# The first two batches of an attention and feed-forward kernel: TensorE's order written out by hand, and SyncE's order of loads

## The chip, the cores and the metric

The kernel runs on one core of a Trainium2 chip. The metric is the device time of one execution in microseconds (us). Before the change it is 924.86 us, the median of 3 runs (923.78 to 927.17). The profiled execution took 924.03 us, and its span in the trace is 922.2 us; the 1.83 us between them lie around the span.

## The reference

For 8 batches of 8 heads (sequence 576, head size 64), attention with two kinds of mask, and then a feed-forward layer over all 4608 tokens:

```python
scores = scale * np.matmul(q, k.transpose(0, 1, 3, 2))
mask_local = (rel >= 0) & (rel < 32)
mask_strided = (rel >= 0) & (pos[None, :] % 32 == pos[:, None] % 32)
# heads 0 to 3: local, heads 4 to 7: strided; softmax over the keys
attn_out = np.matmul(attn, v)
h = x @ w_in                 # x: 4608 x 512, w_in: 512 x 2048
out = (h * np.cos(h)) @ w_out
```

Everything is float32. The products of the feed-forward layer are made from numbers split into a high and a low part, so that one exact product takes three matmuls.

## The kernel before

**The feed-forward layer** works on blocks of 384 tokens and on 16 slices (`f`) of the hidden size. For a block `j` and a slice `f`, `hidden` makes 12 matmuls into bank `a` or `b` (L476), then the cosine curve on ScalarE and VectorE (L482 to L489: scaling, reduction, sine, multiplication by h), then the split into `g_hi` and `g_lo`. `outer` multiplies these with `w_out` in 9 matmuls (L500), three steps (`LAG`) later. Blocks 0 and 1 are worked on together, slice by slice, as their weights arrive; blocks 2 to 5 follow with the attention of batches 2 to 7 laid between their steps; blocks 6 to 11 go through another form (L772, L801).

**The weights** come as 32 tiles of 512 KB (`load_weight`, L144: `raw`, three buffers), two for each slice. ScalarE, VectorE (L158, L161, L167) and GpSimd (L172) turn each into a high and a low part. The n-th load stands behind the load of attention unit 4 + n in SyncE's queue. `put_away` (L591) writes parts of them back to DRAM in 80 stores (L596, L604), for use in the last six blocks.

**The attention** goes in units. A batch has seven: strided, strided, local, strided, strided, local, local (`units`, L422). Here u0 to u6 are the units of batch 0 and u7 to u13 those of batch 1. One unit is: a load of q and k (L297, L352; three buffers `qk`) and of v (L293, L356; five buffers); on TensorE a matmul that lays down the mask (L234) and the score matmuls (L307 local, L367 strided), into one of three banks in turn; the softmax (VectorE L249, L250, ScalarE exponential L261, VectorE L274 to L276, GpSimd L278); a transposition (strided: TensorE L387 and a ScalarE copy L391; local: VectorE L317); the products with v (TensorE L336 local, L401 strided); and copies and splits of the result (`keep`: ScalarE L432, GpSimd L433). Block 0 needs batch 0 alone; block 1 also needs u7, u8, u9, u10 and u11.

**What sets the order.** A scheduler goes through the program with modelled times and puts each engine's instructions into one fixed queue. It takes what is ready in its model and goes by the order of the program otherwise; `order(later, first, ...)` adds an edge that holds the two in sequence. In the attention of batches 0 and 1 (`plain`) TensorE's matmuls have no such edges: `in_stages` and `stage` (L528, L539) only say in which order the program names the stages. Small matmuls on zeros (`keep_busy`, L620, counts in `BUSY`) stand behind the scores of a step. For blocks 0 and 1 the matmuls have no edges either; from block 2 on all matmuls are chained in program order (`in_turn`). SyncE issues all loads and stores named here.

Of the kernel before, what the change touches and what calls it, by code (L numbers as in the profile page):

```python
# [13 lines left out]
F32 = mybir.dt.float32  # L14
# [8 lines left out]
B, H, S, D = 8, 8, 576, 64  # L23
# [22 lines left out]
VL = (LU + 1) * D  # L46
# [11 lines left out]

WEIGHTS_AT, WEIGHTS_EACH = 4, 1

BUSY = (10, 6, 5, 3, 2, 2, 2) + 8 * (1,)


# [23 lines left out]
def attention_cos_ffn(ctx, tc, qkl, vl, qkvs, w_in, w_out, eye, eye16, mask_l0, mask_l, mask_s, out):  # L87
# [114 lines left out]
    class Attention:  # L202
# [6 lines left out]
        def __init__(self, stack, plain, scores, transposed, products, ld_bufs):  # L209

            self.plain = plain
            self.pe = (lambda mm: mm) if plain else in_turn
            self.ld, self.wk = (
                stack.enter_context(tc.tile_pool(name=name, bufs=bufs, side="right", reuse_waits="tile"))
                for name, bufs in (("ld", ld_bufs), ("wk", 2))
            )
            self.scores, self.transposed, self.products = (
                itertools.cycle(kind) for kind in (scores, transposed, products)
            )
            self.turns, self.kept = itertools.cycle(range(len(scores))), {}  # L220
            self.pn_s = itertools.cycle(pn_s)
            self.x_t, self.copied = {}, None
# [5 lines left out]
        def score_bank(self, mask):  # L228


            if self.plain:
                bank = self.bank(self.scores)
                n, w = mask.shape[1:]
                nc.tensor.matmul(  # L234
                    bank[:, :n * w].rearrange("p (t w) -> p t w", w=w), ident16, mask, start=True, stop=False,
                    skip_group_check=True,
                )
                return bank
            n = next(self.turns)
            if n not in self.kept:  # L240
                self.kept[n] = self.bank(self.scores)
                nc.vector.memset(self.kept[n], 0.0)
            return self.kept[n]
# [39 lines left out]
        def stage(self, key):  # L283

            if key not in self.x_t:
                self.x_t[key] = self.wk.tile([P, S], F32, name="x_t")
            return self.x_t[key]

        def local(self, b, u):

            def load_v():
                v = self.ld.tile([P, max(VL, VS)], F32, name="v", bufs=5 if self.plain else 3)
                nc.sync.dma_start(out=v[:, :VL], in_=vl[b, u])  # L293
                return v

            qk = self.ld.tile([P, max(QKL, QS + KS)], F32, name="qk")
            loads.append(nc.sync.dma_start(out=qk[:, :QKL], in_=qkl[b, u]))  # L297
            if self.plain:
                v = load_v()
            q_t = qk[:, :2 * LQ].rearrange("p (h q) -> p h q", h=2)  # L300
# [3 lines left out]

            def score(t, c):
                p, j = divmod(c, 2)
                self.scored = self.pe(nc.tensor.matmul(  # L307
                    s_ps[quarter_of(c), t * KW:(t + 1) * KW], q_t[half(j), p, QB * t:QB * (t + 1)],
                    k_t[half(j), p, QB * t:QB * t + KW], start=not self.plain, stop=True, skip_group_check=True,
                ))  # L310
# [19 lines left out]
            def product(m, c):  # L330


                p, j = divmod(c, 2)
                lo, hi = max(m - 1, 0), min(m + 1, LU)
                at = m * KW - QB if m else 0
                self.pe(nc.tensor.matmul(  # L336
                    a_ps[p][half(j), lo * QB:hi * QB], v_t[quarter_of(c), m], pt[quarter_of(c), at:at + (hi - lo) * QB],
                    start=m == turns[0], stop=m == turns[-1], skip_group_check=True,
                ))
# [9 lines left out]
        def strided(self, b, p, u):  # L349
            real = min(SU, NG - SU * u)  # L350
            qk = self.ld.tile([P, max(QKL, QS + KS)], F32, name="qk")
            loads.append(nc.sync.dma_start(out=qk[:, :QS + KS], in_=qkvs[b, p, u, :, :QS + KS]))  # L352

            def load_v():
                v = self.ld.tile([P, max(VL, VS)], F32, name="v", bufs=5 if self.plain else 3)
                nc.sync.dma_start(out=v[:, :real * D], in_=qkvs[b, p, u, :, QS + KS:QS + KS + real * D])  # L356
                return v

            if self.plain:
# [4 lines left out]
            s_ps = self.score_bank(mask)  # L364

            def score(t, i):
                self.scored = self.pe(nc.tensor.matmul(  # L367
                    s_ps[half(1 - i, GB), t * GB:(t + 1) * GB], q_t[half(i), t], k_t[half(i), t],
                    start=not self.plain, stop=True, skip_group_check=True,
                ))  # L370
# [13 lines left out]
            v_t = v[:, :VS].rearrange("p (t d) -> p t d", d=D)  # L384
            t_ps = self.bank(self.transposed)
            for t in range(0, SU, 2):
                self.pe(nc.tensor.transpose(  # L387
                    t_ps[:, t * GP:(t + 2) * GP], pn[:, t:t + 2].rearrange("p t k -> p (t k)"), ident
                ))
            pt = self.wk.tile([P, SU * GB], F32, name="pt", bufs=2)  # L390
# [7 lines left out]

            def product(t, j):
                at = (t ^ 1) * GB  # L400
                self.pe(nc.tensor.matmul(  # L401
                    a_ps[half(j), t * GB:(t + 1) * GB], v_t[half(j, GB), t], pt[half(j, GB), at:at + GB], start=True,
                    stop=True, skip_group_check=True,
                ))
# [64 lines left out]

    hiddens = itertools.count()  # L470

    def hidden(j, f, x_hi, x_lo):
        h = ps_h.tile([P, 512], F32, name="ab"[next(hiddens) % 2])[:, :TB]
        ops = [(w, x, c) for c in range(NKC) for w, x in ((wi_h, x_hi), (wi_h, x_lo), (wi_l, x_hi))]
        for i, (w, x, c) in enumerate(ops):
            mm = nc.tensor.matmul(h, w[f][:, c], x[c], start=(i == 0), stop=(i == len(ops) - 1))  # L476
            if j >= 2:
                in_turn(mm)

        r = rp.tile([P, TB], F32, name="r")  # L480
# [6 lines left out]
        if j == 0 and f == 0:  # L487
            order(sin, exps[-1], "one change of tables")
        chain["curve"] = nc.vector.tensor_tensor(out=r, in0=r, in1=h, op=ALU.mult)  # L489
        g_hi = gp.tile([P, TB], F32R, name="g_hi")  # L490
        g_lo = gp.tile([P, TB], F32R, name="g_lo")
        chain["cast"] = nc.scalar.copy(out=g_hi, in_=r)  # L492
# [31 lines left out]

    def accumulators(pool):
        return [pool.tile([P, DM], F32, name=f"acc{t}") for t in range(NTT)]

    def in_stages(units, knots, lag):  # L528


        begun = np.interp(range(len(units)), [n for _, n in knots], [at for at, _ in knots]).astype(int).tolist()
        steps = {}
        for n, (at, unit) in enumerate(zip(begun, units)):
            second = min([at + lag] + begun[n + 2:n + 3])
            for stage in (at, second, second + 1):
                steps.setdefault(stage, []).append(unit)
        return steps

    def stage(unit):  # L539

        matmuls = next(unit)
        if matmuls:
            for matmul in matmuls[0]:
                matmul()
            next(unit, None)

    def burst(multiplied, scored):

# [41 lines left out]

    def put_away():  # L591

        for q in range(NQ):
            for i, f, k in ((1, q, 0), (2, q, 1), (5, q + NQ, 1)):
                for part, w in enumerate((wi_h, wi_l)):
                    nc.sync.dma_start(  # L596
                        out=wis[q][i][:, part],
                        in_=w[f][:, 2 * k:2 * k + 2].bitcast(F32).rearrange("p c n -> p (c n)"),
                    )
                if i != 2:  # L600
                    yield
            for f in (q, q + NQ):
                for part, w in enumerate((wo_h, wo_l)):
                    nc.sync.dma_start(out=wos[f][:, part], in_=w[f].bitcast(F32))  # L604
                yield

    direct = {j: x_operands() for j in range(2)}
    with ExitStack() as loading:
        cv = loading.enter_context(tc.tile_pool(name="cv", bufs=3, reuse_waits="tile"))
        with ExitStack() as stack:  # L610
# [3 lines left out]
                stack, True, ((ps_h, "a"), (ps_h, "b"), (ps, "acc0")), ((ps_o, "acc0"), (ps_o, "acc1")),  # L614
                ((ps_o, "acc2"), (ps, "acc3")), ld_bufs=3,
            )
            steps = in_stages(att.units(0) + att.units(1), ((0, 0), (20, 20)), 2)
            spare = ps.tile([P, 512], F32, name="acc2")

            def keep_busy(n, after):  # L620
                for _ in range(n):
                    mm = nc.tensor.matmul(
                        spare[:64], warm, warm.unsqueeze(1).broadcast_to([P, 8, 64]), start=True, stop=True
                    )
                    if after is not None:
                        order(mm, after, "in its place")
                    after = mm

            keep_busy(BUSY[0], None)
            for n in range(max(steps) + 1):  # L630
                for unit in steps.get(n, ()):
                    stage(unit)
                if n + 1 < len(BUSY):
                    keep_busy(BUSY[n + 1], att.scored)

        rp = ctx.enter_context(tc.tile_pool(name="rp", bufs=2, side="right", reuse_waits="tile"))
        gp = ctx.enter_context(tc.tile_pool(name="gp", bufs=LAG + 1, side="right", reuse_waits="tile"))

        with ExitStack() as stack:
# [325 lines left out]
```

## Time and profile before

| | us |
|---|---|
| median of 3 runs | 924.86 |
| profiled execution | 924.03 |
| its span | 922.2 |
| TensorE (PE) busy | 899.3 |
| VectorE (DVE) busy | 525.9 |
| ScalarE (ACT) busy | 520.3 |
| GpSimd (POOL) busy | 434.1 |

Busy times are of the whole span. In rows of engine work, the first number is the start in us from the span's start, the second the duration (of a merged run of instructions), and a bracket at the end gives the engine's idle time just before and what ended it. PEclk is the granted TensorE clock as a share of 2.4 GHz; 0.50 is 1.2 GHz.

### The profile page before, as it was taken

How to read it: one execution, taken by the hardware profiler on the slowest of the kernel's cores; microseconds unless marked ns; L12 is line 12 of the kernel's file. 1: busy time of each engine (PE TensorE's matmuls, PEld its weight loads, DVE VectorE, ACT ScalarE, POOL GpSimd, SP SyncE). 2: the span in 40 equal slices, each digit the busy share in tenths (PEclk: the TensorE clock that was granted, in tenths of full speed). 3: DMA queues.
4: the chain of work that ended last, by engine and by line, in shares of the span. 5: the costliest groups of instructions: out<-in, count | busy, mean ns of one | idle time of the engine just before them, and what ended most of it. 6: DMA issues, size and time to landing. Idle time of an engine off the chain costs nothing. (4 is left out here: it accounts for less than half of the span.)

```text
span 922.2 us, 20559 instructions
## 1 busy us (share of the span) xinstructions
PE 899.3 (98%) x7876; PEld 790.0 (86%) x7876; DVE 525.9 (57%) x1018; ACT 520.3 (56%) x1090; POOL 434.1 (47%) x466
## 2 busy tenths in 40 slices
PE   8789999999999999999999999999999999999998
PEld 5568999988888888888888888999898998999896
DVE  5658665446657666666664345646464555544453
ACT  3556777556567666656655544545555555544443
POOL 2636655544666666656746523424333434323231
PEclk9889999999999999999999999999999999999999
DMA  8938876322336535544355755756576655755401
GB/s 307 309 100 300 267 234 216 125 88 77 118 128 193 188 132 165 194 150 142 130 176 173 259 178 168 228 175 215 191 265 200 199 187 182 253 183 193 138 23 68
DMA packets 93265, 166.33 MB, mean 180 GB/s; under 512 B 10736, under 2 KB 34032, under 8 KB 93168
## 3 DMA queue, kind: packets, MB, share of 16 engines
q1 hardware_dynamic: 85248, 157.72, 52.1%
q10 hardware_dynamic: 7920, 7.31, 2.4%
q8 instruction: 62, 1.02, 0.4%
q14 instruction: 35, 0.29, 0.1%
HBM read 125.40 MB, written 39.58 MB: 179 GB/s over the span
## 5 line engine op out<-in xcount | busy, mean ns | idle before, releaser
L787 POOL TENSOR_TENSOR g_lo<-r,g_hi 128x384 fp32r<-128x384 f32 x96 | 98.8, 1029 | 247.7 <-ACT g_hi L786 139.3
L493 POOL TENSOR_TENSOR g_lo<-r,g_hi 128x384 fp32r<-128x384 f32 x96 | 103.5, 1078 | 186.1 <-ACT g_hi L492 108.8
L500 PE MATMUL acc<-s,g_hi 128*128 128x512 f32 x576 | 180.0, 396 | 0.0
L801 PE MATMUL acc<-s,g_hi 128*128 128x512 f32 x576 | 179.7, 393 | 0.0
L500 PEld LDWEIGHTS acc<-s,g_hi 128*128 128x128 f32 x576 | 105.3, 188 | 15.5
L801 PEld LDWEIGHTS acc<-s,g_hi 128*128 128x128 f32 x576 | 106.2, 188 | 10.8
L801 PE MATMUL acc<-s,g_lo 128*128 128x512 f32 x288 | 112.8, 392 | 0.0
L500 PE MATMUL acc<-s,g_lo 128*128 128x512 f32 x288 | 110.9, 390 | 0.0
L476 PE MATMUL b<-x_hi,s 128*128 128x384 f32 x384 | 109.3, 345 | 1.1 <-DVE r L489 1.1
L781 DVE SCALAR_TENSOR_TENSOR r<-r,h 128x384 f32<-128x384 int32 x96 | 58.3, 607 | 90.9 <-ACT r L780 90.8
L476 PE MATMUL a<-x_hi,s 128*128 128x384 f32 x384 | 109.2, 345 | 0.7 <-DVE r L489 0.7
L772 PE MATMUL a<-s,s 128*128 128x384 f32 x384 | 83.1, 338 | 0.0
L783 DVE TENSOR_TENSOR r<-r,h 128x384 f32<-128x384 f32 x96 | 69.9, 728 | 22.0 <-ACT r L782 20.3
L782 ACT ACTIVATE r<-r,biases 128x384 f32<-128x384 f32 x96 | 59.2, 617 | 36.8 <-DVE r L781 36.5
L486 ACT ACTIVATE r<-r,biases 128x384 f32<-128x384 f32 x96 | 58.8, 612 | 30.3 <-DVE r L483 28.5
L476 PEld LDWEIGHTS b<-x_hi,s 128*128 128x128 f32 x384 | 70.9, 190 | 4.6 <-DVE r L489 1.9
L786 ACT CAST g_hi<-r 128x384 fp32r<-128x384 f32 x96 | 49.1, 512 | 44.0 <-DVE r L783 43.6
L476 PEld LDWEIGHTS a<-x_hi,s 128*128 128x128 f32 x384 | 70.4, 188 | 3.6 <-DVE r L489 1.0
L780 ACT ACTIVATE r<-h 128x384 int32<-128x384 f32 x96 | 50.4, 525 | 39.9 <-DVE h L850 26.3
L772 PEld LDWEIGHTS a<-s,s 128*128 128x128 f32 x384 | 69.4, 188 | 4.2
L492 ACT CAST g_hi<-r 128x384 fp32r<-128x384 f32 x96 | 49.1, 511 | 29.9 <-DVE r L489 27.9
L476 PE MATMUL b<-x_lo,s 128*128 128x384 f32 x192 | 64.8, 338 | 0.0
(141 smaller groups left out, 1757.9 us busy)
## 6 DMA issues: line engine op xcount, KB each, us to landing
s<-wis SPq DMA_DIRECT2D x168, 256.0 KB, 2.9
s<-wos SPq DMA_DIRECT2D x96, 256.0 KB, 3.5
qk<-in_qkvs SPq DMA_DIRECT2D x32, 324.0 KB, 3.6
qk<-in_qkl SPq DMA_DIRECT2D x24, 416.0 KB, 3.9
out<-o SPq DMA_DIRECT2D x36, 256.0 KB, 2.4
raw<-in_w_in SPq DMA_DIRECT2D x16, 512.0 KB, 5.6
raw<-in_w_out SPq DMA_DIRECT2D x16, 512.0 KB, 3.9
wos<-s SPq DMA_DIRECT2D x32, 256.0 KB, 5.4
```

Source lines behind the costliest of these rows:

```text
L476: mm = nc.tensor.matmul(h, w[f][:, c], x[c], start=(i == 0), stop=(i == len(ops) - 1))
L486: sin = nc.scalar.activation(out=r, in_=r, func=AF.Sin, bias=quarter)
L492: chain["cast"] = nc.scalar.copy(out=g_hi, in_=r)
L493: chain["rest"] = nc.gpsimd.tensor_tensor(out=g_lo, in0=r, in1=g_hi.bitcast(F32), op=ALU.subtract)
L500: mm = nc.tensor.matmul(acc[t], g[:, ts], w[f], start=(f == 0 and i == 0), stop=(f == NFC - 1 and i == 2))
L772: in_turn(nc.tensor.matmul(bank, w[:, n, c], part, start=start and i == 0, stop=stop and i == len(ops) - 1, skip_group_check=True,))
L780: nc.scalar.activation(out=k, in_=h, func=AF.Copy, scale=1.0 / (2.0 * math.pi), bias=0.25)
L781: nc.vector.scalar_tensor_tensor(out=r, in0=k, scalar=-2.0 * math.pi, in1=h, op0=ALU.mult, op1=ALU.add)
L782: nc.scalar.activation(out=r, in_=r, func=AF.Sin, bias=quarter)
L783: chain["curve"] = nc.vector.tensor_tensor(out=r, in0=r, in1=h, op=ALU.mult)
L787: chain["rest"] = nc.gpsimd.tensor_tensor(out=g_lo, in0=r, in1=g_hi.bitcast(F32), op=ALU.subtract)
L801: in_turn(nc.tensor.matmul(acc, g[gn][:, ts], w[wn], start=done == 0 and i == 0, stop=done == NFC - 1 and i == 2,))
```

## The change

TensorE's matmuls of the first two batches are all chained with `in_turn`, the small matmuls on zeros too, in an order that the program writes out: at step n the scores of unit n, the matmuls on zeros, the products of unit n - 4, and the transposition of unit n - 3. After the last scores, the weights of slices 0 and 1 are asked for, and the remaining four products follow; ahead of the last two of them (those of u12 and u13) stand the 12 matmuls each of block 0's slices 0 and 1, with their curves. `hidden` takes these two results where it made them itself before. The pool `rp` is opened earlier for this.

In SyncE's queue, loads for the attention units of batches 2 to 7 now stand behind the last weight load, and the stores of `put_away` behind the latest attention load that the program has named by then, which is one of batches 2 to 7.

```diff
+PRODUCT_LAG, TRANSPOSE_LAG = 4, 3
...
-                nc.sync.dma_start(out=v[:, :VL], in_=vl[b, u])
+                load = nc.sync.dma_start(out=v[:, :VL], in_=vl[b, u])
+                if not self.plain:
+                    order(load, tiles[-1], "weights first")
...
-    def hidden(j, f, x_hi, x_lo):
+    begun_early = 2 * [None]
+
+    def curved_inputs(j, f, x_hi, x_lo):
...
-            if j >= 2:
+            if j >= 2 or f < len(begun_early) and j == 0:
                 in_turn(mm)
...
+    def hidden(j, f, x_hi, x_lo):
+        r = begun_early[f] if j == 0 and f < len(begun_early) else curved_inputs(j, f, x_hi, x_lo)
...
+        def put(out, part):
+            order(nc.sync.dma_start(out=out, in_=part), loads[-1], "units first")
...
-            steps = in_stages(att.units(0) + att.units(1), ((0, 0), (20, 20)), 2)
+            units = att.units(0) + att.units(1)
...
+            def run(unit):
+                for matmul in next(unit)[0]:
+                    matmul()
+
+            keep_busy(BUSY[0])
+            for n, unit in enumerate(units):
+                run(unit)
                 if n + 1 < len(BUSY):
-                    keep_busy(BUSY[n + 1], att.scored)
+                    keep_busy(BUSY[n + 1])
+                if n >= PRODUCT_LAG:
+                    run(units[n - PRODUCT_LAG])
+                    next(units[n - PRODUCT_LAG], None)
+                if n >= TRANSPOSE_LAG:
+                    next(units[n - TRANSPOSE_LAG])
+                next(unit)
+            need_weights(cv, 1)
+            for n, unit in enumerate(units[-PRODUCT_LAG:], len(units)):
+                if n - PRODUCT_LAG >= len(units) - len(begun_early):
+                    f = n - PRODUCT_LAG - len(units) + len(begun_early)
+                    begun_early[f] = curved_inputs(0, f, *direct[0])
+                run(unit)
+                next(unit, None)
+                if n < len(units) + TRANSPOSE_LAG:
+                    next(units[n - TRANSPOSE_LAG])
```

## Rows read from the trace of the kernel before

**Rows 1.** The page: busy time of TensorE, and its busy tenths in 40 slices of the span.

```profile
PE 899.3 (98%) x7876; PEld 790.0 (86%) x7876; DVE 525.9 (57%) x1018; ACT 520.3 (56%) x1090; POOL 434.1 (47%) x466
...
PE   8789999999999999999999999999999999999998
```

**Rows 2.** Busy time in stretches: bounds, length, then busy us (and instructions) of PE, PEld, DVE, ACT, POOL; granted clock, DMA share, GB/s.

```profile
0.00:80.00 80.00, 66.30 (x1128) 49.71 (x1129) 50.72 (x113) 41.09 (x97) 36.42 (x45) 0.91 0.74 245
...
200.00:260.00 60.00, 60.00 (x768) 52.44 (x767) 37.44 (x87) 39.28 (x88) 32.66 (x40) 1.00 0.33 104
```

**Rows 3.** The same columns for the first 64 us, finer.

```profile
18.00:22.00 4.00, 3.33 (x125) 2.25 (x120) 4.00 (x9) 3.70 (x10) 3.12 (x3) 1.00 1.03 337
22.00:26.00 4.00, 2.60 (x50) 1.78 (x50) 4.00 (x10) 2.09 (x6) 4.00 (x6) 1.00 0.90 336
26.00:30.00 4.00, 2.68 (x51) 1.90 (x49) 4.00 (x9) 3.20 (x8) 3.99 (x4) 1.00 0.99 349
30.00:34.00 4.00, 1.84 (x46) 1.60 (x46) 3.92 (x11) 2.15 (x7) 2.74 (x3) 0.84 1.04 333
34.00:38.00 4.00, 4.00 (x122) 3.61 (x122) 0.21 (x2) 2.13 (x8) 3.33 (x5) 0.50 0.93 334
...
60.00:62.00 2.00, 2.00 (x9) 2.00 (x8) 0.00 (x0) 0.47 (x3) 0.00 (x0) 0.50 0.57 168
```

**Rows 4.** The same columns for two longer stretches.

```profile
0.00:34.00 34.00, 27.40 (x491) 16.97 (x493) 24.22 (x61) 16.16 (x37) 16.58 (x22) 0.98 0.93 321
34.00:58.30 24.30, 19.15 (x502) 14.79 (x498) 11.38 (x30) 10.09 (x33) 10.60 (x16) 0.82 0.47 158
```

**Rows 5.** TensorE's instructions in order of time: products of u4, products of u5 and u6, scores of u9, scores of u13, matmuls on zeros, products of u11, first part of block 0, products of u13, block 0 again, the end of its slice 1, and the start of block 1.

```profile
30.21 0.79 PE L401 MATMUL acc<-pt,v 54*64 54x54 f32 x20 [0.17 <-ACT pt L391]
...
33.49 3.19 PE L336 MATMUL acc<-pt_l,v 32*64 32x32 f32 x100 [2.00 <-ACT x_t L409]
...
37.45 1.51 PE L307 MATMUL a<-qk 64*32 64x64 f32 x48
...
50.67 0.55 PE L387 MATMUL acc<-ident,pn_s 128*128 128x128 f32 x3
51.05 0.33 PE L234 MATMUL b<-ml,ident 128*128 128x384 bf16 x1
51.31 0.88 PE L307 MATMUL b<-qk 64*32 64x64 f32 x48
52.11 0.40 PE L622 MATMUL acc<-warm 128*64 128x512 bf16 x1
52.45 0.79 PE L401 MATMUL acc<-pt,v 54*64 54x54 f32 x20
...
58.47 1.02 PE L336 MATMUL acc<-pt_l,v 32*64 32x32 f32 x56 [2.50 <-DVE pt_l L317]
59.42 0.62 PE L476 MATMUL a<-x_hi,s 128*128 128x384 f32 x2
...
64.22 0.34 PE L476 MATMUL b<-x_hi,s 128*128 128x384 f32 x1
65.21 0.44 PE L476 MATMUL a<-x_hi,s 128*128 128x384 f32 x1 [0.66 <-DVE r L489]
```

**Rows 6.** The chain that ended last, one piece: 12 matmuls of one slice at the full clock.

```profile
530.12 2.12 PE b L476 x12
```

**Rows 7.** VectorE in order of time: the first and the last instruction of u13.

```profile
53.70 0.52 DVE L249 TENSOR_REDUCE mx<-b 128x6 f32<-128x384 f32 x1
...
57.63 0.58 DVE L317 STREAM_TRANSPOSE pt_l<-t_sb 128x384 f32<-128x384 f32 x1 [1.19 <-POOL t_sb L278]
```

**Rows 8.** VectorE's preparation of the weights: two single instructions of L161, and the groups of L161 and L167 in the first 64.6 us (count, busy us, mean ns).

```profile
14.43 0.69 DVE L161 SCALAR_TENSOR_TENSOR bits<-raw,bits 128x512 int32<-128x512 int32 x1
...
23.24 1.37 DVE L161 SCALAR_TENSOR_TENSOR bits<-raw,bits 128x512 int32<-128x512 int32 x1
```

```profile
L161 DVE SCALAR_TENSOR_TENSOR bits<-raw,bits 128x512 int32<-128x512 int32 x6 | 5.6, 956 | 0.3 <-ACT bits L153 0.3
...
L167 DVE SCALAR_TENSOR_TENSOR bits<-raw,bits 128x512 int32<-128x512 int32 x4 | 2.8, 698 | 0.0
```

**Rows 9.** The stores of `put_away` (L596, L604) and the weight loads (L144) by line, over the whole span: count, duration in ns (least, median, most), first and last start in us.

```profile
L596 SPq DMA_DIRECT2D wis<-s x48: 319/359/1100, 18.4 to 172.7; - x48
...
L604 SPq DMA_DIRECT2D wos<-s x32: 319/340/630, 23.5 to 171.4; - x32
...
L144 SPq DMA_DIRECT2D raw<-in_w_out x16: 327/333/432, 11.6 to 160.4; - x16
```

**Rows 10.** DMA issues up to 43.5 us: count, KB each, median us to landing.

```profile
wis<-s SPq DMA_DIRECT2D x8, 128.0 KB, 5.5
wos<-s SPq DMA_DIRECT2D x4, 256.0 KB, 5.5
```

**Rows 11.** Attention of the later batches: SyncE's issue of a load for a strided unit, the first score matmul that reads it, the first scores of batch 2, and the time to landing of such loads between 200 and 300 us.

```profile
230.26 0.33 SPq L352 DMA_DIRECT2D qk<-in_qkvs  x1
...
241.19 0.25 PE L367 MATMUL acc<-qk 64*54 64x54 f32 x1
...
202.32 0.81 PE L367 MATMUL acc<-qk 64*54 64x54 f32 x24
```

```profile
qk<-in_qkvs SPq DMA_DIRECT2D x9, 324.0 KB, 3.0
```

More of the change, by code (lines that the diff above doesn't have):

```diff
@@ L211, in __init__ @@
             self.plain = plain
-            self.pe = (lambda mm: mm) if plain else in_turn
             self.ld, self.wk = (
@@ L233, in score_bank @@
                 n, w = mask.shape[1:]
-                nc.tensor.matmul(
+                in_turn(nc.tensor.matmul(
                     bank[:, :n * w].rearrange("p (t w) -> p t w", w=w), ident16, mask, start=True, stop=False,
                     skip_group_check=True,
-                )
+                ))
                 return bank
@@ L297, in local @@
             loads.append(nc.sync.dma_start(out=qk[:, :QKL], in_=qkl[b, u]))
+            if not self.plain:
+                order(loads[-1], tiles[-1], "weights first")
             if self.plain:
@@ L306, in score @@
                 p, j = divmod(c, 2)
-                self.scored = self.pe(nc.tensor.matmul(
+                in_turn(nc.tensor.matmul(
                     s_ps[quarter_of(c), t * KW:(t + 1) * KW], q_t[half(j), p, QB * t:QB * (t + 1)],
@@ L335, in product @@
                 at = m * KW - QB if m else 0
-                self.pe(nc.tensor.matmul(
+                in_turn(nc.tensor.matmul(
                     a_ps[p][half(j), lo * QB:hi * QB], v_t[quarter_of(c), m], pt[quarter_of(c), at:at + (hi - lo) * QB],
@@ L352, in strided @@
             loads.append(nc.sync.dma_start(out=qk[:, :QS + KS], in_=qkvs[b, p, u, :, :QS + KS]))
+            if not self.plain:
+                order(loads[-1], tiles[-1], "weights first")
             def load_v():
                 v = self.ld.tile([P, max(VL, VS)], F32, name="v", bufs=5 if self.plain else 3)
-                nc.sync.dma_start(out=v[:, :real * D], in_=qkvs[b, p, u, :, QS + KS:QS + KS + real * D])
+                load = nc.sync.dma_start(out=v[:, :real * D], in_=qkvs[b, p, u, :, QS + KS:QS + KS + real * D])
+                if not self.plain:
+                    order(load, tiles[-1], "weights first")
                 return v
@@ L366, in score @@
             def score(t, i):
-                self.scored = self.pe(nc.tensor.matmul(
+                in_turn(nc.tensor.matmul(
                     s_ps[half(1 - i, GB), t * GB:(t + 1) * GB], q_t[half(i), t], k_t[half(i), t],
@@ L386, in strided @@
             for t in range(0, SU, 2):
-                self.pe(nc.tensor.transpose(
+                in_turn(nc.tensor.transpose(
                     t_ps[:, t * GP:(t + 2) * GP], pn[:, t:t + 2].rearrange("p t k -> p (t k)"), ident
@@ L400, in product @@
                 at = (t ^ 1) * GB
-                self.pe(nc.tensor.matmul(
+                in_turn(nc.tensor.matmul(
                     a_ps[half(j), t * GB:(t + 1) * GB], v_t[half(j, GB), t], pt[half(j, GB), at:at + GB], start=True,
@@ L489, in hidden @@
         chain["curve"] = nc.vector.tensor_tensor(out=r, in0=r, in1=h, op=ALU.mult)
+        return r
+    def hidden(j, f, x_hi, x_lo):
+        r = begun_early[f] if j == 0 and f < len(begun_early) else curved_inputs(j, f, x_hi, x_lo)
         g_hi = gp.tile([P, TB], F32R, name="g_hi")
@@ L526, in accumulators @@
         return [pool.tile([P, DM], F32, name=f"acc{t}") for t in range(NTT)]
[L528 to L545, printed above, removed]
     def burst(multiplied, scored):
@@ L595, in put_away @@
                 for part, w in enumerate((wi_h, wi_l)):
[L596 to L599, printed above, removed]
+                    put(wis[q][i][:, part], w[f][:, 2 * k:2 * k + 2].bitcast(F32).rearrange("p c n -> p (c n)"))
                 if i != 2:
@@ L603, in put_away @@
                 for part, w in enumerate((wo_h, wo_l)):
-                    nc.sync.dma_start(out=wos[f][:, part], in_=w[f].bitcast(F32))
+                    put(wos[f][:, part], w[f].bitcast(F32))
                 yield
     direct = {j: x_operands() for j in range(2)}
+    rp = ctx.enter_context(tc.tile_pool(name="rp", bufs=2, side="right", reuse_waits="tile"))
     with ExitStack() as loading:
@@ L616, in attention_cos_ffn, with keep_busy @@
             )
-            steps = in_stages(att.units(0) + att.units(1), ((0, 0), (20, 20)), 2)
+            units = att.units(0) + att.units(1)
             spare = ps.tile([P, 512], F32, name="acc2")
-            def keep_busy(n, after):
+            def keep_busy(n):
                 for _ in range(n):
-                    mm = nc.tensor.matmul(
+                    in_turn(nc.tensor.matmul(
                         spare[:64], warm, warm.unsqueeze(1).broadcast_to([P, 8, 64]), start=True, stop=True
[L624 to L632, printed above, removed]
-                if n + 1 < len(BUSY):
-                    keep_busy(BUSY[n + 1], att.scored)
-        rp = ctx.enter_context(tc.tile_pool(name="rp", bufs=2, side="right", reuse_waits="tile"))
+                    ))
+            def run(unit):
[4 more added lines that the diff above has]
+                run(unit)
+                if n + 1 < len(BUSY):
+                    keep_busy(BUSY[n + 1])
[14 more added lines that the diff above has]
+                    next(units[n - TRANSPOSE_LAG])
         gp = ctx.enter_context(tc.tile_pool(name="gp", bufs=LAG + 1, side="right", reuse_waits="tile"))
```

## The prediction

> **What bounds the kernel now.** I read the page's busy times and slices first, then busy time by stretches, then TensorE's order of time in the stretch with gaps, and last the other engines and SyncE there. On the page the reader is to see that TensorE is busy 899.3 of 922.2 us, and that the digits below 9 stand at the very start and end [rows 1]. By stretches, 80 - 66.3 = 13.7 us of its 22.9 us of idle time lie in the first 80 us; the other 9.2 us are spread over 842 us, and 200 to 260 us, as one of the later stretches, has none [rows 1, 2]. So nearly all later work follows back to back, and a microsecond won before 65 us is won at the end.
>
> What limits that start changes at 34 us. From 18 to 34 us VectorE is busy 15.92 of 16 us, and the DMA engines are full too (333 to 349 GB/s, share 0.90 to 1.04) [rows 3]. From 34 to 58.3 us VectorE does 11.38 us of work in 24.3 us and the DMA share is 0.47 [rows 4]: nothing but the order is full there. TensorE's rows show the order: the products of u4 end at 31.0 us, those of u5 and u6 then hold the head of its queue until 36.7 us, and the scores of u9 start at 37.45 us only [rows 5]. Meanwhile VectorE, which has to have scores to work on, stands at 0.21 busy of 4 us, and TensorE itself runs at a granted clock of 0.50, its 1.2 GHz level, after having been busy only 1.84 of the 4 us before [rows 3].
>
> I measure the start by one mark: the end of everything up to block 0's slice 1, products of u13 included. Before, it is 64.22 + 0.34 = 64.56 us [rows 5].
>
> **The change part by part.** *Scores ahead.* Nothing of the attention's computation is removed. In the new order the scores of u9 stand right behind the products of u4 (step 8), so they can start at about 31.0 us if the first 31 us stay as they are; the products of u5 and u6 follow behind the scores of u9 and u10. From there two chains run.
>
> VectorE's chain: it is full up to 34 us, then has 11.38 us of work left [rows 4], mostly that of the five units u9 to u13, 2.3 us each. With three to four units scored ahead, I let it be full to 0.9, a little under the share of the stretch before. Its last unit takes 57.63 + 0.58 - 53.70 = 4.51 us from the first instruction to the end of the last [rows 7], since it waits for ScalarE and GpSimd. So 34 + (11.38 - 2.3) / 0.9 + 4.5 = 48.6 us, and with the products of u13, 1.02 us [rows 5], 49.6 us.
>
> TensorE's chain, at full clock, from 31.0 us: five steps of mask 0.33, scores 0.88, one matmul on zeros 0.40, products 0.79 to 1.02, and in three of them a transposition of 0.55 [rows 5]; the rows overlap by some 0.07 us each, so about 2.6 us a step and 13.2 us for u9 to u13. Then products of u10 and u11 with one transposition (0.9 + 0.55 + 0.8), two times 2.1 us for block 0's slices [rows 6], two times 0.95 for the last products: 8.3 us. That ends at 31.0 + 13.2 + 8.3 = 52.5 us.
>
> The longer one is TensorE's, 52.5 us. Two chains that wait for each other don't run without gaps, so I add 2 us: 54.5 us. The bounds: without any gap 52.5 us; and if the middle of the start keeps every wait that it has now, only the tail is gained (next paragraph), 60.5 us.
>
> *Block 0 ahead of the last products.* Before, five of the 24 matmuls ran ahead of u13's products, TensorE waited 2.50 us for u13's transposition, and the other 19 then took from 59.42 to 64.56 us, 5.1 us, at a granted clock of 0.50 in part [rows 3, 5]. Behind u12's scores and u13's softmax these 24 matmuls are cover: 4.2 us at the full clock fit into the time from u13's scores at 51.31 to its transposition at 58.21 us [rows 5, 7]. So even with an unchanged attention the mark comes at about 58.2 + 0.25 + 1.02 + up to 1 us, 60 to 60.5 us: 4 us gained. That is part of the 10 us, not on top of it. The curve of slice 0 is then done by the time of the mark, so the wait of 0.66 us of block 1 [rows 5] should go; I count it as nothing, since the sine must still wait for u13's exponential.
>
> *Stores moved away from the start.* 12 stores of `put_away` are issued before 43.5 us, 8 x 128 + 4 x 256 KB = 2.05 MB [rows 10]; at the 335 GB/s of that time they take 6 us of a full DMA. This gain is inside the assumption that loads keep up with scores 6 us earlier; without it they would not. All 80 stores, 14.3 MB by the sizes of the rows, last issued at 172.7 us [rows 9, 10], now come after 200 us, where the DMA moves 104 GB/s at a share of 0.33 [rows 2]. They are named over 32 steps, each of at least 12 matmuls of 2.12 us [rows 6] and nine wider ones that take about as long: over 134 us or more they add at most 107 GB/s, so there is room. Price: zero to the time in the slower rival.
>
> *Later units behind the weights.* The last weight load is issued at 160.4 us [rows 9], the first scores of batch 2 stand at 202.32 us [rows 11]: 42 us for a load that lands in 3.0 us [rows 11]. Hidden; if this cover were gone it would cost one landing, 3 us, once.
>
> *The small matmuls.* Same count, now in the chain; nothing.
>
> Sum: 64.56 - 54.5 = 10.1 us less at the mark, and nothing gained or lost behind it. 924.03 - 10.1 = 913.9 us for the profiled execution. That execution is 0.83 us under the median of the runs shown, so I forecast 914.8 us.
>
> One rule of the Trainium skill speaks against it. VectorE's L161 takes 0.69 us alone at 14.43 us and 1.37 us at 23.24 us, where GpSimd is busy all 4 us; six of them take 5.6 us in place of 4.1 [rows 3, 8]. The page "SBUF — State Buffer" (section "Who interferes with whom") says that a VectorE instruction with two SBUF inputs and a GpSimd instruction that reads SBUF shut each other out for a whole instruction. The trace agrees for L161. A denser start puts more of both beside each other, which is the second rival.
>
> **The rivals.** *Only the tail is gained.* The chain of matmuls now stops as a whole at a late transposition or product: u5's and u6's wait of 2.00 us before 33.49 us [rows 5] was such a stop, and now the scores of u9 to u13 stand behind others. For it: the matmuls wait for softmaxes that VectorE, full to 34 us, delivers late. Against it: the scores lead by three units, so VectorE keeps work while TensorE waits. Gain 4 us: 921 us.
>
> *VectorE gets longer.* If all ten L161 and L167 before the mark took the 1.37 us of the slow one, in place of 5.6 us for six and 2.8 us for four [rows 8], that is 13.7 - 8.4 = 5.3 us on the engine that is full to 34 us. The gain falls to 4.8 us: 920 us. The rule of the Trainium skill's page "SBUF — State Buffer", section "Who interferes with whom", would at worst come to this.
>
> *Full gain.* No gaps, the wait of 0.66 us gone and loads earlier by the 2 MB, so that u0 to u8 are ahead of 31.0 us by 2 to 3 us: 14 us, 911 us or a little less.
>
> *Slower: the stores now hold up the attention of the later batches.* SyncE's queue is one line, and a qk load there has two buffers. A load issued at 230.26 us is read at 241.19 us [rows 11]: 10.9 us, of which landing takes 3.0, so it decides from a delay of about 7.9 us on. By the knots in the code some 26 units are scored in the 32 steps in which the stores are named. If half of them came 1.5 us late at TensorE, that is 20 us lost against 10 won: 935 us; from 0.8 us each on the result is slower than before. Against it: a store needs about 0.34 us of the queue [rows 9], and the DMA is two thirds idle there [rows 2].
>
> *The order doesn't bind.* The scheduler's model may have had much the same order, or loads may be late by the DMA's full share: 924 us.
>
> **How the numbers follow.** Chances: forecast 0.55 (910 to 919), only the tail 0.16, VectorE longer 0.06, full gain 0.09, slower 0.09, no change 0.05. What a measurement of this kernel can tell from no change is about 0.5%, 4.6 us: faster means under 920.2 us. The forecast and the full gain lie there, and of the two half gains a little less than half: 0.73. Within: 0.18. Slower: 0.09. The range leaves out the slower rival and the far end of the full gain: 909 to 925 us.
>
> **What would show it.** In the trace of after: the scores of u9 at about 31 us and of u13 at 42 to 44 us; VectorE without a stretch of 4 us at 0.21 between 30 and 48 us; the mark at 52 to 57 us, with no wait for u13's transposition; no stores to DRAM by L596 or L604 before 200 us; from there to the end the same length as before within 1.5 us. The prediction is wrong if the mark comes after 60 us (the chain stops as a whole), or if TensorE's idle time between 200 and 400 us grows by more than 2 us (the stores).

## The result and the profile after

The changed kernel takes 929.56 us (median of 6 runs, 928.62 to 930.74) against 924.17 us (median of 6) of the kernel before on the same chip: ratio 1.0051, 95% interval 1.0037 to 1.0066. It is slower by 4.7 us going by the ratio, where 10 us less were forecast. The profiled execution took 928.94 us with a span of 927.2 us, 5.0 us more than before.

Busy time by stretches, columns as in [rows 2], for the whole start, the stretches of [rows 4], and 200 to 260 us:

```profile
0.00:80.00 80.00, 63.57 (x1098) 47.16 (x1099) 48.53 (x111) 40.73 (x96) 35.62 (x45) 0.85 0.56 187
...
200.00:260.00 60.00, 60.00 (x671) 52.46 (x670) 35.72 (x81) 38.18 (x81) 29.57 (x37) 1.00 0.56 180
```

```profile
0.00:34.00 34.00, 26.79 (x471) 16.46 (x475) 23.75 (x59) 15.17 (x34) 16.38 (x22) 0.94 0.84 289
34.00:58.30 24.30, 19.25 (x462) 14.91 (x462) 12.02 (x31) 10.68 (x34) 10.18 (x17) 0.78 0.32 100
```

The idle time in the first 80 us rose from 13.7 to 80 - 63.57 = 16.4 us, and the mean granted clock there fell from 0.91 to 0.85. At 200 to 260 us TensorE is full as before, although the DMA now moves 180 GB/s there in place of 104; from 200 to 400 us it is idle for 1.3 us, where it was 1.4. TensorE's waits, over the whole span (us in total, times, longest), with the line of the kernel before that the first one answers to:

```profile
PE acc L409 <- ACT pt L399: 10.2, 6, 3.8
PE b L486 <- DVE r L499: 4.2, 1, 4.2
PE acc L395 <- ACT x_l L349: 3.2, 5, 1.4
```

```profile
PE acc L401 <- ACT pt L391: 1.5, 2, 1.3
```

The first line is the attention's products waiting for ScalarE's copies `pt` of transposed scores; all six lie before 56 us. The second is one wait, right behind the start. The third lies behind 80 us and was 3.9 us before. Where the first two lie is seen in TensorE's order of time (L375, L311 scores; L395 transposition; L409, L340 products; L486 block 0 and 1):

```profile
26.71 0.55 PE L395 MATMUL acc<-ident,pn_s 128*128 128x128 f32 x3
...
32.25 1.32 PE L409 MATMUL acc<-pt,v 54*64 54x54 f32 x20 [3.79 <-ACT pt L399]
...
33.94 1.51 PE L311 MATMUL a<-qk 64*32 64x64 f32 x48
...
42.66 0.91 PE L409 MATMUL acc<-pt,v 54*64 54x54 f32 x24 [1.33 <-ACT pt L399]
...
47.75 0.88 PE L311 MATMUL b<-qk 64*32 64x64 f32 x48
...
53.46 1.09 PE L409 MATMUL acc<-pt,v 54*64 54x54 f32 x24 [3.19 <-ACT pt L399]
...
55.90 1.32 PE L409 MATMUL acc<-pt,v 54*64 54x54 f32 x20 [0.52 <-ACT pt L399]
57.15 0.69 PE L486 MATMUL a<-x_hi,s 128*128 128x384 f32 x1
...
64.34 1.02 PE L340 MATMUL acc<-pt_l,v 32*64 32x32 f32 x56
65.29 0.44 PE L486 MATMUL a<-x_hi,s 128*128 128x384 f32 x1
...
71.82 0.69 PE L486 MATMUL b<-x_hi,s 128*128 128x384 f32 x1 [4.18 <-DVE r L499]
```

The scores did come earlier: u9's at 33.94 in place of 37.45 us, u13's at 47.75 in place of 51.31 [rows 5]. But the mark (the end of everything up to slice 1 and u13's products) is 64.34 + 1.02 = 65.36 us, against 64.56 before: the 3.6 us are lost again between u13's scores and the mark. Slice 0's matmuls, behind the waits of 3.19 and 0.52 us, run at the lower clock (first row). Behind the mark TensorE stands still for 4.18 us, and the stretch after that is at the lower clock again:

```profile
58.00:60.00 2.00, 2.00 (x8) 2.00 (x7) 0.00 (x0) 0.10 (x1) 0.59 (x1) 0.50 0.27 98
...
66.00:68.00 2.00, 1.65 (x10) 1.33 (x8) 0.11 (x1) 1.60 (x5) 1.75 (x2) 1.00 0.69 203
68.00:70.00 2.00, 0.00 (x0) 0.00 (x0) 1.01 (x2) 0.69 (x3) 0.77 (x1) 1.00 0.94 333
...
72.00:74.00 2.00, 2.00 (x7) 2.00 (x8) 1.31 (x2) 2.00 (x6) 1.47 (x2) 0.50 0.44 90
74.00:76.00 2.00, 2.00 (x8) 2.00 (x7) 1.04 (x3) 1.46 (x3) 2.00 (x2) 0.50 0.94 334
```

Both kinds of wait go back to ScalarE, the second by way of VectorE's last step of the curve. ScalarE's order of time at the two places:

```profile
30.54 0.47 ACT L261 ACTIVATE t_sb<-t_sb 128x324 f32<-128x324 f32 x1 [2.27 <-DVE t_sb L250]
30.92 0.46 ACT L417 COPY x_t<-acc 128x324 f32<-128x324 f32 x1
31.26 0.62 ACT L172 CAST s<-bits 128x512 fp32r<-128x512 f32 x1
31.77 0.43 ACT L399 COPY pt<-acc 128x324 f32<-128x324 f32 x1
...
64.10 1.25 ACT L167 ACTIVATE raw<-raw 128x512 f32<-128x512 f32 x2
...
66.07 0.31 ACT L348 COPY x_l<-acc 128x192 f32<-128x192 f32 x1
66.28 0.62 ACT L172 CAST s<-bits 128x512 fp32r<-128x512 f32 x1
...
66.80 0.32 ACT L349 COPY x_l<-acc 128x192 f32<-128x192 f32 x1
...
67.52 0.49 ACT L492 ACTIVATE r<-b 128x384 int32<-128x384 f32 x1 [0.40 <-ACT x_l L349]
69.32 0.66 ACT L154 ACTIVATE bits<-raw 128x512 int32<-128x512 uint32 x1 [1.30 <-DMA raw<-in_w_out]
69.88 0.60 ACT L496 ACTIVATE r<-r,biases 128x384 f32<-128x384 f32 x1
...
71.94 0.52 ACT L506 CAST g_hi<-r 128x384 fp32r<-128x384 f32 x1
```

At the first place, u4's transposition ends at 27.26 us on TensorE, but its copy (31.77) stands in ScalarE's queue behind the exponential of u7 (30.54), for which VectorE is not ready, while ScalarE is idle for 2.27 us. At the second, slice 1's matmuls end at 64.4 us, but its first curve step (67.52) stands behind the two copies of u12's products (66.07, 66.80), which the change put behind slice 0, and behind four instructions on weight tiles between 64.10 and 66.90 us; its sine (69.88) stands behind a weight tile whose load lands only then. Nor could `outer` fill the gap: slice 0's curve was done at 64.79 us, but its `g_hi`, which `outer` needs, was cast only at 71.94 us, behind the copies of u13.

That gave three theories. **A**: the early place of block 0 is the fault (second wait, lower clock). **B**: the written-out chain is the fault, since the whole of TensorE now stops at a copy that ScalarE has in a late place (the six waits). **C**: SyncE's edges are the fault.

### The profile page after: what moved, and what is told of

It reads as the page before. It is cut to its first block, busy times and chain, and to the rows that moved or that the text cites. A ratio compares the mean times of both kernels' runs of the same rounds, so it can differ in the third digit from the quotient of the medians.

```text
span 927.2 us, 20516 instructions
## 1 busy us (share of the span) xinstructions
PE 902.5 (97%) x7876; PEld 793.1 (86%) x7876; DVE 520.9 (56%) x1018; ACT 521.8 (56%) x1090; POOL 433.2 (47%) x466
## 3 DMA queue, kind: packets, MB, share of 16 engines
q8 instruction: 62, 1.02, 0.5%
## 5 line engine op out<-in xcount | busy, mean ns | idle before, releaser
L486 PE MATMUL b<-x_hi,s 128*128 128x384 f32 x384 | 110.0, 347 | 4.2 <-DVE r L499 4.2
L486 PE MATMUL a<-x_hi,s 128*128 128x384 f32 x384 | 109.9, 347 | 0.0
L486 PEld LDWEIGHTS b<-x_hi,s 128*128 128x128 f32 x384 | 71.3, 191 | 7.2 <-DVE r L499 4.5
L486 PEld LDWEIGHTS a<-x_hi,s 128*128 128x128 f32 x384 | 71.3, 190 | 2.7
L486 PE MATMUL a<-x_lo,s 128*128 128x384 f32 x192 | 65.2, 339 | 0.0
```

## The experiments

Each ratio is to the kernel before on the same chip in the same round of runs (medians 924.00 to 924.92 us). Where runs are compared with each other below, it is by these ratios.

| run | median us | ratio to before (95%) |
|---|---|---|
| the change | 929.56 | 1.0051 (1.0037 to 1.0066) |
| a1 products first | 926.27 | 1.0016 (1.0004 to 1.0028) |
| a2 SyncE undone | 931.09 | 1.0070 (1.0055 to 1.0085) |
| a3 SyncE alone | 924.61 | 0.9995 (0.9981 to 1.0009) |
| a4 sine first | 929.01 | 1.0045 (1.0030 to 1.0060) |
| b1 copies first | 924.96 | 1.0008 (0.9994 to 1.0022) |
| b2 products and copies first | 921.38 | 0.9971 (0.9960 to 0.9983) |
| b3 curves first | 926.30 | 1.0029 (1.0017 to 1.0041) |
| b4 curves and copies first | 921.91 | 0.9972 (0.9960 to 0.9984) |
| c1 before, copies first | 927.54 | 1.0031 (1.0017 to 1.0045) |
| c2 as b2, SyncE undone | 922.42 | 0.9978 (0.9967 to 0.9989) |

**a1, products first.** Block 0's slices 0 and 1 behind the last products, in the chain:

```diff
-                if n - PRODUCT_LAG >= len(units) - len(begun_early):
-                    f = n - PRODUCT_LAG - len(units) + len(begun_early)
-                    begun_early[f] = curved_inputs(0, f, *direct[0])
                 run(unit)
...
+            for f in range(len(begun_early)):
+                begun_early[f] = curved_inputs(0, f, *direct[0])
```

> The changed kernel with one thing moved back: block 0's first two products stand behind the last local units' products again, still in the written-out chain. Theory A (the early place of block 0 is the fault: it pushes the products of u12 and u13, their ScalarE copies and with them the sine of slice 1 back, so that TensorE waits 4.2 us and then runs at 1.2 GHz): the wait of 4.18 us before the third product of block 0 is gone, its start comes at about 66 us in place of 71.8, and the time is 922 to 925 us, that of the kernel before or a little less. Theory B (the written-out chain with scores leading is the fault: six waits for ScalarE's pt copies, 10.2 us): no change, 928 to 930 us. Theory C (SyncE's edges are the fault): no change, 928 to 930 us.

Measured 926.27 us: 0.0035 of the ratio, 3.2 us, come back. The wait before slice 2 is gone; what is left of waits for curves is 1.75 and 1.0 us:

```profile
PE acc L409 <- ACT pt L399: 11.6, 6, 3.3
...
PE a L486 <- DVE r L499: 1.7, 1, 1.7
...
PE b L486 <- DVE r L499: 1.0, 1, 1.0
```

Theory A holds, but not alone: the median is 1.3 us above the 922 to 925 us expected, 1.5 us stay against the kernel before, and the waits for copies are as large as ever. Slice 2 starts at 73.94 us, not at about 66 us. One reason is that `outer` of slice 0 now stands in front of it. The other is that this execution was late from the start: up to the products of u11 the written-out order is that of the change, but they start at 59.10 us in place of 55.90, and VectorE's first instruction on a weight tile (L159), which waits for its load, at 15.50 us in place of 13.84. So marks of single executions can differ by 3 us where the order is the same, and between runs the medians decide.

**a2 and a3, SyncE's edges.** a2 takes all the edges `"weights first"` and `"units first"` of `put` out of the change, a3 puts them alone into the kernel before.

> The changed kernel without the edges on SyncE's loads and stores (loads of later batches not held behind the weights, stores of put_away not held behind the loads). Theories A and B: 928 to 930 us, the wait of about 4 us before the third product of block 0 stays. Theory C: 923 to 925 us.

> The kernel before with SyncE's edges alone. Theories A and B: 923 to 925.5 us, as before, with the DMA below 200 GB/s instead of 245 GB/s in the first 80 us. Theory C: 928 to 930 us.

Without them the change gains nothing: 931.09 us lies even above the 928 to 930 us that A and B allowed, on the other side from C. Alone they change nothing (0.9995). The DMA in the first 80 us of a3 is 187 GB/s in place of 245, as expected. Theory C falls.

**a4, sine first.** In `load_weight`, for a `w_out` tile of slice f; `sine` is that of block 0's slice f - 2, `first` ScalarE's L154:

```diff
+            if sine is not None:
+                order(first, sine, "sine first")
```

> The changed kernel with one edge more on ScalarE: the first instruction on a w_out weight tile stands behind the sine of two slices earlier, so the sine of slice 1 no longer waits for a weight load. Theory A, if the load in front of the sine is what sets the wait: the wait of 4.18 us falls to 2 to 3 us, 925 to 928 us. Theory A, if the late copies of u12 and u13 set it: the wait stays at 3.5 us or more, 928 to 930 us. Theories B and C: 928 to 930 us.

In the profiled execution the wait is 2.15 us, as theory A has it, and no lower clock follows; but that execution, 927.31 us, was the fastest of four, and the median of 929.01 us isn't told apart from the change and lies where B and C had it. By itself this run settles nothing.

**b1, copies first.** In `softmax`, for batches 0 and 1:

```diff
                 exps.append(nc.scalar.activation(out=e, in_=t, func=AF.Exp, scale=0.125))
+                if self.copied is not None:
+                    order(exps[-1], self.copied, "copies first")
```

> The changed kernel with one edge more on ScalarE for each attention unit: its exponential stands behind the copies that the program names before it (so the pt copy that the next products wait for no longer stands behind an exponential whose scores come later). Theory B (the chain stops at pt copies, 10.2 us in six waits, because ScalarE has them behind a later exponential): these waits fall to 5 us or less, block 0 starts 4 to 5 us earlier, and the time falls to 924 to 926 us. Theory B2 (the copies are late because VectorE and GpSimd are late, not by ScalarE's order): waits for the copies stay at 9 us or more, and the time at 928 to 930 us. The wait of about 4 us before the third product of block 0 is not touched by this edge and should stay.

Measured 924.96 us, 0.0043 of the ratio, 4.0 us less than the change. The waits:

```profile
PE acc L411 <- ACT pt L401: 6.9, 5, 2.2
PE b L488 <- DVE r L501: 4.2, 1, 4.2
```

The copies' waits fall from 10.2 to 6.9 us, less than expected, and the 4.2 us behind block 0's slices stay, as expected. u4's copy now stands in front of u7's exponential, at 33.27 us, and waits behind an instruction on a weight tile instead, which waits for VectorE:

```profile
32.74 0.62 ACT L172 CAST s<-bits 128x512 fp32r<-128x512 f32 x1 [2.23 <-DVE bits L168]
33.27 0.42 ACT L401 COPY pt<-acc 128x324 f32<-128x324 f32 x1
```

The products of u10 wait 0.98 us in place of 3.19. With that, u12's products start at 57.17 us in place of 61.11. Theory B holds in the time, with A's fault still in; of the waits it explains a third.

**b2, both repairs** (a1's and b1's edits together).

> Both repairs at once: copies ahead of exponentials, and block 0's first two products behind the last local units' products. If theory A (early place, 3 us) and theory B (late copies, 4 us) are both right and add up: 921 to 923 us, faster than the kernel before. If the early place was the only fault: 925.5 to 927 us, as in the run with the products first.

Measured 921.38 us, 0.9971 of the kernel before. If the two faults simply add, 1.0051 - 0.0035 - 0.0043 = 0.9973 was to come. Slice 1 and all products now end at 61.33 + 0.34 = 61.67 us, 2.9 us ahead of before, and the span is 920.2 us, 2.0 us less; in between TensorE waits for the curve of slice 0:

```profile
50.85 0.91 PE L411 MATMUL acc<-pt,v 54*64 54x54 f32 x24 [1.04 <-ACT pt L401]
...
53.25 1.27 PE L411 MATMUL acc<-pt,v 54*64 54x54 f32 x20 [1.01 <-ACT pt L401]
54.45 2.86 PE L342 MATMUL acc<-pt_l,v 32*64 32x32 f32 x112
57.23 0.44 PE L488 MATMUL a<-x_hi,s 128*128 128x384 f32 x1
...
61.33 0.34 PE L488 MATMUL b<-x_hi,s 128*128 128x384 f32 x1
64.19 0.44 PE L488 MATMUL a<-x_hi,s 128*128 128x384 f32 x1 [2.52 <-DVE r L501]
```

The mark is still 7.2 us behind the 54.5 us of the forecast. The waits for copies have not gone:

```profile
PE acc L411 <- ACT pt L401: 7.2, 5, 2.0
```

In three of the five (1.78, 1.40 and 2.00 us, those of u1, u3 and u4) ScalarE's copy stands behind instructions on weight tiles that wait for a load or for VectorE. No run moves these, so what the rest of the forecast gain would take stays open.

**b3 and b4, curves first.** Block 0 stays in its early place; the copies of u12 and u13 stand behind the sine of slice 1 on ScalarE, a4's edge is in, and `gp`, the pool of `g_hi` and `g_lo`, is opened ahead of the attention; b4 has b1's edge too.

```diff
+    gp = ctx.enter_context(tc.tile_pool(name="gp", bufs=LAG + 1, side="right", reuse_waits="tile"))
     with ExitStack() as loading:
...
+                    if f:
+                        next(units[-2], None)
                 run(unit)
-                next(unit, None)
+                if unit is not units[-2]:
+                    next(unit, None)
...
+            if self.plain and len(sines) == len(begun_early):
+                for copy in copies:
+                    order(copy, sines[-1], "sine first")
```

> The changed kernel with block 0 left in its early place, and ScalarE's order mended there: the copies of u12 and u13 and the weight instructions of two slices later stand behind the sine of slice 1, and the pool of g_hi and g_lo is opened early, so that they wait for no memory of the attention. Theory A in its form by ScalarE's order: the wait before the third product of block 0 falls from 4.18 us to 1 us or less, and the time to 924.5 to 926.5 us. If the early place hurts by something else (the clock, the weights of slice 2): still 928 us or more.

> The last one with the copies ahead of the exponentials too. Theories A and B together: 919 to 922 us, the full gain less some of it. If only the early place mattered: as the run with the curves first alone.

In b3 no wait for a curve is left in the start; one of 1.4 us for u13's late copies has come:

```profile
PE acc L416 <- ACT pt L406: 11.0, 6, 3.8
PE acc L402 <- ACT x_l L352: 3.5, 6, 1.4
PE acc L523 <- ACT x_l L352: 1.4, 1, 1.4
```

The median, 926.30 us, is at the upper end of what A expected, and 2.0 us (0.0022) better than the change, with intervals that overlap a little. (b3's profiled execution, 929.18 us, is the slowest of its nine.) With the copies first, b4 reaches 921.91 us, as b2 does. So the early place of block 0, once ScalarE's order suits it, is worth as much as the late one and no more. In b3 `outer` of slice 0 (74.09 us) also stands in front of slice 2 (75.60 us), as in a1; how much of the gain is this, the copies or the weight instructions isn't separated.

**c1 and c2.** c1 is b1's edge in the kernel before; c2 is b2 without SyncE's edges.

> The kernel before, with nothing of the change, and the one edge on ScalarE (an exponential stands behind the copies named before it). If that edge is worth its 4 us by itself: 920 to 922 us. If it repairs only what the written-out chain makes late (there the whole of TensorE stops at a late copy, in the kernel before the scheduler lays other matmuls in front): 923 to 926 us.

> Written-out chain, products first, copies first, but SyncE's order as in the kernel before (no edges for later batches' loads and the stores of put_away). If SyncE's edges give something once TensorE's order no longer hides it (the stores take DMA time in the first 34 us): 922.5 to 924.5 us against 921.4 with them. If they give nothing: 921 to 922 us.

c1 is slower than the kernel before, 1.0031, which neither expectation had: without the written-out chain the same edge does harm. The gain of b2 is thus the chain and the edge together. In c1's trace TensorE is not idle for longer, but its clock is lower; in the stretch of [rows 4] it is busy 20.76 us in place of 19.15, at 0.64 in place of 0.82:

```profile
34.00:58.30 24.30, 20.76 (x456) 16.19 (x456) 13.37 (x35) 11.08 (x35) 12.02 (x17) 0.64 0.49 153
```

What lowers it there stays open. c2 at 922.42 us lies 1 us above b2, inside both intervals, and a2 lies 1.5 us above the change; whether SyncE's edges give anything stays open.

## Why the prediction was wrong

*What bounds the start: right.* TensorE is full behind 80 us but for the last stretch and short waits, and the start decides.

*Scores ahead: right in direction.* u9's scores came at 33.94 us (31 forecast), u13's at 47.75 (42 to 44), and u13's transposition on VectorE ended 3.5 us earlier:

```profile
50.42 0.52 DVE L249 TENSOR_REDUCE mx<-b 128x6 f32<-128x384 f32 x1
...
54.17 0.58 DVE L321 STREAM_TRANSPOSE pt_l<-t_sb 128x384 f32<-128x384 f32 x1 [1.01 <-POOL t_sb L278]
```

That is 54.75 us against 58.21 [rows 7], where I had put 48.6.

*The step that failed first is TensorE's chain "at full clock" with 2 us added for all waits.* The mark came 65.36 - 54.5 = 10.9 us late, behind the 60 us that I had named as the sign of a chain that stops as a whole. Up to u9's scores 2.9 us were lost, mostly the wait of 3.79 us for u4's copy; from there to u13's scores 13.8 us passed where four steps of 2.6 were put, 3.4 us more, with a wait of 1.33 us and matmuls at the lower clock (u9's scores, at a granted clock of 0.50, take 1.51 us for the 0.88 put); from u13's scores to the mark 17.6 us, where the forecast without its margin of 2 us had 52.5 - 31.0 - 10.4 = 11.1 us, so 6.5 us more. In that last piece 3.19 + 0.52 us are waits for copies, and slice 0 takes 57.15 to 61.11, 4.0 us, at the 1.2 GHz level for the 2.1 us that I took from a row at the full clock. My upper bound of 60.5 us took the waits of the old order as the worst case; the new order brought its own, 10.2 us for copies in place of 1.5. I had named the chain's stops as a rival ("only the tail is gained") and put the cause on VectorE. b1 shows the cause that I had not looked at: ScalarE's queue, on which copies of old units and exponentials of new ones stand in an order that the scheduler chose by its own times. b1 and b2 show this for part of the waits only; the copies behind weight instructions are read from the traces, not moved by a run. That the kernel before waits less for copies because the scheduler laid other matmuls in front of them is my reading of its order, not shown.

*The second is "nothing gained or lost behind" the mark.* I wrote that slice 0's curve would be done by then, and looked no further. Slice 1's curve was not: the change moved u12's and u13's products behind block 0's matmuls, and with them their ScalarE copies into the way of slice 1's curve and of slice 0's `g_hi`, beside the weight instructions there. From the mark to the end 927.2 - 65.36 = 861.8 us passed, against 857.6 before: 4.2 us, of which the wait of 4.18 us and about 2 us for 12 matmuls at the lower clock (71.82 to 75.83 us) are the body; on the other side stand the waits of 0.66 and 1.12 us that the kernel before had there. By a1 and b3 this is worth 2.0 to 3.2 us.

*The tail's gain of 4 us* did not come: a1, b3 and b4 show that the early place brings nothing against the late one. u13's transposition (54.75 us) was done before TensorE reached block 0 (57.15 us), so there was no gap left to cover. The term was taken from the order before, in which the gap existed.

*The stores and the later loads: right.* TensorE's time at 200 to 260 us is untouched, a3 shows no cost, and the slower rival, which I had put there, has no part in the loss. Six stores came already at 167 to 170 us, not after 200. The result lies on that rival's side by another mechanism.

*VectorE longer:* not seen at L161, for which the prediction cited the Trainium skill's page "SBUF — State Buffer", section "Who interferes with whom". Its six instructions up to the mark (L162 now) take 4.8 us, where they took 5.6 [rows 8]. The 14 small instructions L275, of which the last section shows one, take 4.7 us in place of 3.6, so the two nearly cancel.

## What to carry to other kernels

When one engine's order is written out by hand, every instruction on the other engines that it waits for needs a place as well: here one late copy on ScalarE stopped all of TensorE. For each wait in the new order, look at what stands ahead of the releasing instruction in its own queue, and write that edge too; here one edge on ScalarE was worth 4 us in the chain, more than the margin put aside for all waits, and cost 2.9 us in the kernel without the chain. Work moved forward pushes other work back, and what must be checked is who waits for the work pushed back: its copies, its memory, the curve behind it.

## Not expected of the hardware

A VectorE instruction on 6 values for each partition (L275), 0.16 to 0.17 us when alone, took 1.21 us beside a GpSimd instruction of 1.25 us that ran at the same time (VectorE, then GpSimd, in the changed kernel):

```profile
28.84 1.21 DVE L275 TENSOR_SCALAR z<-z 128x6 f32<-128x6 f32 x1
...
41.91 0.17 DVE L275 TENSOR_SCALAR z<-z 128x6 f32<-128x6 f32 x1
```

```profile
28.76 1.25 POOL L173 TENSOR_TENSOR s<-bits,s 128x512 fp32r<-128x512 f32 x1
```

It ends 0.04 us behind the GpSimd instruction. So the smallest step of a softmax can cost seven times its time, and the forecast had no term for it.
